# Two leftover expert jobs: six of their eight weight slices go from native FP32 matmuls to split operands, with both parts of the activation side by side

## The chip, the cores and the metric

One core of a Trainium2 chip runs the whole kernel. The metric is the device time of one launch in microseconds; three runs of the kernel before gave 592.71, 593.57 and 594.28. The trace comes from one profiled execution of its own.

## The reference, cut to what matters

A block-wise linear attention gives 1536 rows of 512 values. A first mixture of 8 experts sends each row to its best expert, a second one sends each row to its two best. An expert is `h = max(x @ w1, 0)`, then `out[mask] += weight * (h @ w2)`, with `w1` 512x1024 and `w2` 1024x512 in FP32:

```python
for e in range(E):
    for k in range(2):
        mask = top2[:, k] == e
        h = np.maximum(x[mask] @ w1[e], 0.0)
        out[mask] += top2_w[mask, k, None] * (h @ w2[e])
```

## The kernel before, in words

Behind the attention, the work is a list of 18 jobs: one expert with a fixed number of rows each (its columns, `c`). Jobs 0 to 7 are the first mixture (184 to 224 columns), jobs 8 and 9 take 256 rows of experts 0 and 1 of the second, and the rest of these two experts, 160 columns each, are the **leftover jobs**, which stand as job 10 and job 14 in the order. Jobs 11, 12, 13 and 15 have 416, 408, 400 and 392 columns, jobs 9, 16 and 17 multiply by rows.

A job has 8 steps, one for each 128 of the 1024 hidden units. Steps are numbered through, s = 8 j + f, so job 10 is steps 80 to 87 and job 14 steps 112 to 119. Step s emits, in this order: the hidden product h(s) (`hstep`: four matmul groups, one for each 128 of the 512 inputs, d = 0 to 3) with its relu; the output product y(s-2) (`ystep`, LAG = 2); in f = 1 the copy of the finished output of the job before (`ycopy`); weight loads (`wload`, issued from ACT's queue); the transposes of the next job's rows (`xprep`, in f = 4 to 7 for a job of four blocks, block b = d) and the scaled output rows of the job before (`post2`, `put_rows`); last the split of the weights of step s+3 (`split`, LEAD = 3). Each engine takes its instructions in this order.

Split operands: `split` writes the high part of a weight slice rounded to fp32r (h1, h2: two ACT copies of 128x512) and the rest in bf16 (l1, l2: two DVE subtractions). `xprep` and `hstep` do the same with x (xs) and with the hidden values (hs): high part first, low part behind it in one tile of 2c columns. A product is then high weight times high part, high weight times low part and low weight times the high part in bf16. In `high`, with `side` false the first two are two matmuls of c columns, each with its own weight load; with `side` true they are one matmul of 2c columns, whose two halves must be added afterwards. Before, `side` is true for the output products of jobs 0 to 7 alone, where `ycopy` adds the halves (L810, L811).

The leftover jobs have all eight steps in `raw`: no split, weights straight from the load buffer (r), x as FP32 (xf), native FP32 matmuls (L740), and one ACT relu (hf, L757). The h tile in PSUM has two buffers, so h(s) starts only when the readers of h(s-2) are done; y tiles have one each. When `wload` may refill a load buffer that a leftover job uses is worked out in lines 1216 to 1219 from the raw steps: three steps later than elsewhere, since the last raw slice of a half is read by y(s) two steps on.

Of the kernel before, what the change touches and what calls it, by code (L numbers as in the profile page):

```python
# [8 lines left out]
FT = mybir.dt.float32  # L9
# [5 lines left out]
AF = mybir.ActivationFunctionType  # L15
# [13 lines left out]
KD = DM // 128  # L29
NF = F // 128  # L30
STAT1 = (224, 224)
RANK1 = (224, 216, 208, 200, 192, 184)
EARLY2 = 256
STAT2 = (416, 416)
# [4 lines left out]
CR = max(STAT2[:2]) - EARLY2  # L39
# [11 lines left out]
NJOIN = 2  # L51
OUT_ROWS = N + TRASH
RAWB = 3
LAG = 2
LAST = 3
LEAD = 3
# [29 lines left out]
class Job:  # L86


    def __init__(self, ly, c, e=None, r=None, t0=0, row=False, raw=()):
        self.ly, self.e, self.r, self.t0, self.c, self.row = ly, e, r, t0, c, row  # L90
        self.raw = raw
        self.nt = -(-c // 128)
        self.wr = (W1R, W2R)[ly]

# [5 lines left out]
def emit(ctx, tc, kq, kv, lam, moe_expert_emb, moe_tau, moe_w1, moe_w2, moe2_w_gate, moe2_w_noise,  # L100
         moe2_noise, moe2_w1, moe2_w2, out):
    nc = tc.nc
# [187 lines left out]
    JOBS = [Job(0, c, e=e) for e, c in enumerate(STAT1)]  # L290
    JOBS += [Job(0, c, r=r) for r, c in enumerate(RANK1)]
    JOBS += [Job(1, EARLY2, e=e, row=True) for e in range(2)]
    rest = [Job(1, c, r=r, row=c <= ROWS) for r, c in enumerate(RANK2)]
    rest += [Job(1, STAT2[e] - EARLY2, e=e, t0=EARLY2 // 128, raw=range(NF)) for e in range(2)]
    JOBS += [rest[i] for i in ORDER2]
    NJ = len(JOBS)
    NSTEP = NJ * NF
# [3 lines left out]
    def wload(u, eng=nc.sync):  # L301
# [15 lines left out]
        f0 = half * 512  # L317
        r1 = wts.tile([128, KD, 512], FT, name="r1", bufs=RAWB)
        eng.dma_start(r1, w1[e].rearrange("o (k p) f -> p (o k) f", p=128)[:, :, f0:f0 + 512])
        r2 = wts.tile([128, 4, DM], FT, name="r2", bufs=RAWB)  # L320
        eng.dma_start(r2, w2[e].rearrange("o (k p) f -> p (o k) f", p=128)[:, f0 // 128:f0 // 128 + 4])
# [5 lines left out]
    def drip(n=1):  # L327
        for _ in range(min(n, len(small))):
            fn, *a = small.pop(0)
            fn(*a)  # L330

    def split(s):
# [10 lines left out]
        h1 = wts.tile([128, KD, 128], FR, name="h1", bufs=LEAD + 1)  # L343
        h2 = wts.tile([128, DM], FR, name="h2", bufs=LEAD + 2 + LAG)
        l1 = wts.tile([128, KD, 128], BF, name="l1", bufs=LEAD + 1)
        l2 = wts.tile([128, DM], BF, name="l2", bufs=LEAD + 2 + LAG)
        nc.scalar.activation(h1, a1, AF.Copy)  # L347
# [211 lines left out]
    XS = {}  # L559
# [88 lines left out]
    mo = moe.enter_context(tc.tile_pool(name="mo", bufs=2))  # L648
# [5 lines left out]
    def table1():  # L654

        pr = pm.tile([128, 512], FT, name="t", bufs=2)
        for i in JOIN:
            pa, pb = RR[i]
            nc.tensor.matmul(pr[:, :E * NT], pa, pb, start=i == JOIN[0], stop=i == NTI - 1)
        nc.vector.tensor_add(tab1, tab1, pr[:, :E * NT].rearrange("p (e t) -> p e t", t=NT))  # L660
        window_index(0, tab1[:, :S1, :T1], g1[:, :S1], ok1[:, :S1])
        gather(1)
        gather(0)
        window1(slice(0, S1))
# [71 lines left out]
    def products(c, ops, side=False, low_first=False):  # L736

        if ops[0][2] is None:
            for o, w, _, mov, first, last in ops:
                nc.tensor.matmul(o[:, :c], w, mov, start=first, stop=last, skip_group_check=True)  # L740
            return
        a, b = (low, high) if low_first else (high, low)
        for op in ops:
            a(c, op, side, op[4], False)
        for op in ops:
            b(c, op, side, False, op[5])

    def hstep(s):
        j, f = divmod(s, NF)
        jb = JOBS[j]  # L750
        c = jb.c
        h1, l1, _, _ = SPLIT[s]
        ph = pm.tile([128, 512], FT, name="h", bufs=2)
        if l1 is None:
            products(c, [(ph, h1[:, d, :], None, XS[j][1][:, d, :c], d == 0, d == KD - 1) for d in range(KD)])
            hf = mo.tile([128, CR], FT, name="hf", bufs=LAG + 1)
            nc.scalar.activation(hf[:, :c], ph[:, :c], AF.Relu)  # L757
            HS[s] = hf[:, :c]
            drip(2)
            return  # L760
        products(c, [(ph, h1[:, d, :], l1[:, d, :], XS[j][0][:, d, :], d == 0, d == KD - 1) for d in range(KD)])
        hs = mo.tile([128, 2 * C2], FR, name="hs", bufs=LAG + 2)
        hh, hl = hs[:, :c], hs[:, c:2 * c]
        HS[s] = hs[:, :2 * c]
        nc.scalar.activation(hh, ph[:, :c], AF.Relu)  # L765
        nc.vector.scalar_tensor_tensor(hl, ph[:, :c], 0.0, hh.bitcast(FT), op0=OP.max, op1=OP.subtract)  # L766
        drip()

    def row_product(s, t):
        j, f = divmod(s, NF)  # L770
        _, _, h2, l2 = SPLIT[s]
        hh, hl = (HS[s][:, o + t * 128:o + (t + 1) * 128] for o in (0, JOBS[j].c))
        nc.tensor.matmul(PY[j][t], hh, h2, start=f == 0, stop=False)  # L773
        nc.tensor.matmul(PY[j][t], upper_half(hh), l2, start=False, stop=False)  # L774
        nc.tensor.matmul(PY[j][t], hl, h2, start=False, stop=f == NF - 1)  # L775

    def ystep(s):
        j, f = divmod(s, NF)
        if f == 0:
            PY[j] = [pm.tile([128, 512], FT, name=f"y{d}") for d in range(KD)]  # L780
        _, _, h2, l2 = SPLIT[s]
        w = [slice(d * 128, (d + 1) * 128) for d in range(KD)]
        ops = [(PY[j][d], h2[:, w[d]], None if l2 is None else l2[:, w[d]], HS[s],
                f == 0, f == NF - 1) for d in range(KD)]
        if JOBS[j].row:
            last = s >= NSTEP - LAST
            if last and f < NF - 1:
                return
            for t in range(JOBS[j].nt):
                for x in range(s - LAST + 1 if last else s, s + 1):  # L790
                    row_product(x, t)
                if last:
                    put_rows(j, t, PY[j][t], 128)
        else:
            products(JOBS[j].c, ops, not JOBS[j].ly, low_first=True)
        del SPLIT[s], HS[s]

    def ycopy(j):
        jb = JOBS[j]
        c = jb.c  # L800
        if jb.row:
            for t in range(jb.nt):
                put_rows(j, t, PY[j][t], 128)
            return
        yt = yts.rearrange("p (d c) -> p d c", d=KD) if jb.ly else yt1
        YT[j] = yt
        for d in range(KD):
            o = yt[:, d, :c]
            if not jb.ly:
                nc.scalar.activation(o, PY[j][d][:, c:2 * c], AF.Copy)  # L810
                nc.vector.tensor_add(o, PY[j][d][:, :c], o)  # L811
            elif d % 2:
                nc.scalar.activation(o, PY[j][d][:, :c], AF.Copy)
            else:
                nc.vector.tensor_copy(o, PY[j][d][:, :c])  # L815
# [209 lines left out]
    def put_rows(j, t, src, p):  # L1025

        w, ix = Q[j]
        row = mo.tile([128, DM], FT, name="orow", bufs=4)
        if t % 2:
            nc.scalar.activation(row[:p], src[:p], AF.Copy, scale=w[:p, 0, t:t + 1])  # L1030
        else:
            nc.vector.tensor_scalar(row[:p], src[:p], w[:p, 0, t:t + 1], None, op0=OP.mult)  # L1032
        nc.gpsimd.memset(spacer, 0.0)
        s = nc.gpsimd.indirect_dma_start(  # L1034
            out=out[:, :], out_offset=bass.IndirectOffsetOnAxis(ap=ix[:p, t:t + 1], axis=0),
            in_=row[:p], in_offset=None, compute_op=OP.add)
        for o in scat3.setdefault(j, []):
            tc.declare_no_dep(s.ins, o.ins, reason="rows of other tokens")
        scat3[j].append(s)
# [176 lines left out]
    for u in range(len(WLOADS), 2 * NJ):  # L1216
        raw = [f % 4 for f in JOBS[(u - 3) // 2].raw if f // 4 == (u - 3) % 2 and u >= 3]
        s = max(0, 4 * (u - 3) + max([WF] + [x + LAG for x in raw]))
        loads.setdefault(s, []).append(u)

    table1()
    for s in range(NSTEP + LAG):
        j, f = divmod(s, NF)
        if s < NSTEP:
            hstep(s)

        if s >= LAG and not (f == LAG and 0 < j <= E):
            if f == LAG + 1 and 0 < j <= E:
                ystep(s - LAG - 1)
            ystep(s - LAG)  # L1230
        if f == LAG - 1 and j and not (j == NJ and JOBS[-1].row):
            ycopy(j - 1)
        for u in loads.get(s, ()):
            wload(u, nc.scalar)
        if 12 <= s < 12 + 4 * 8 and s % 4 == 0:
            zero_out(s // 4 - 3)
        for fn, a in sorted(todo.get((j, f), ()), key=lambda x: (post1_e, pe_0, pe_1).index(x[0]) if x[0] in (post1_e, pe_0, pe_1) else 3):
            if fn in stages:
                drip(99)
            fn(*a)  # L1240
        split(s + LEAD)
# [225 lines left out]
```

## Time and profile before

| what | us |
| --- | --- |
| median of three runs | 593.57 |
| profiled execution, whole | 598.39 |
| its span, first to last instruction | 596.6 |
| PE busy | 570.7 |
| DVE busy | 379.5 |
| ACT busy | 294.9 |
| mean granted TensorE clock | 0.984 |

A row of the timeline has the start in us from the span's start, the time, engine, line, operation, tiles and shape. Times of one instruction run from its start to its end in the pipeline; the next on the same engine often starts sooner, so the cost of one in a row of many is the distance between two starts. L740 counts two instructions for one FP32 matmul: a group "x8" is the four products of one step.

### The profile page before, as it was taken

Reading aid. Unit: us, or ns where it says so; the run is one execution under the profiler, and the core shown is the slowest. Engines: PE = TensorE matmul, PEld = TensorE weight load, DVE = VectorE, ACT = ScalarE, POOL = GpSimd, SP = SyncE. Lnnn points to the kernel's source line nnn. Section 1 sums busy time; section 2 is a strip of 40 time slices with the busy share of each in tenths; the row PEclk is TensorE's granted clock in tenths of the full one; section 3 lists DMA queues with packets and bytes.
Section 4 is the critical chain, followed back from the end, with each engine's and each line's share of the span. In section 5 each row is a group of like instructions: output and inputs, shape, how many; then the busy total and the mean of one; then the engine's idle time right before and its main releaser. Section 6 shows DMA issues by size and latency. Waiting matters only on the chain.

```text
span 596.6 us, 11448 instructions
## 1 busy us (share of the span) xinstructions
PE 570.7 (96%) x4216; PEld 482.8 (81%) x4217; DVE 379.5 (64%) x1162; ACT 294.9 (49%) x696; POOL 211.3 (35%) x408
## 2 busy tenths in 40 slices
PE   5999779999999999999999999999999999999992
PEld 3898669999999998897778887887879988777761
DVE  3688759788888888878851644665632364655520
ACT  3566326776677667676531534435331444435310
POOL 5786434423624523233355131032132613031303
PEclk9899799999999999999999999999999999999997
DMA  6999139867787775765687585165435776261404
GB/s 215 377 301 388 76 101 373 314 228 254 282 316 251 253 264 178 264 232 178 213 236 203 192 301 185 28 170 182 149 49 197 187 257 203 103 176 20 53 1 57
DMA packets 56353, 119.40 MB, mean 200 GB/s; under 512 B 4973, under 2 KB 6549, under 8 KB 56290
## 3 DMA queue, kind: packets, MB, share of 16 engines
q10 hardware_dynamic: 38208, 75.60, 36.2%
q0 software_dynamic: 9360, 25.38, 16.5%
q1 hardware_dynamic: 8722, 17.62, 8.5%
q8 instruction: 35, 0.57, 0.4%
q14 instruction: 28, 0.23, 0.1%
HBM read 100.50 MB, written 18.09 MB: 199 GB/s over the span
## 4 chain that ended last, share of the span: by engine, by line
PE 86%; DMA 4%; DVE 3%; POOL 1%; ACT 1%; issue 1%; SPq 1%; POOLq 0%; DVEq 0%
PE h L729 12%; PE h L730 11%; PE h L734 10%; PE y L727 8%; PE y L734 8%; PE y L730 4%; PE y L729 4%; PE t L710 4%; PE h L740 3%; PE y L740 3%; PE y L774 2%; PE y L775 2%; PE y L773 2%; DMA xw<-x,g 2%; PE px L431 2%; PE pa L376 2%
## 5 line engine op out<-in xcount | busy, mean ns | idle before, releaser
L729 PE MATMUL h<-xs,h 128*128 128x224 f32 (+11 forms) x512 | 148.6, 314 | 0.0
L730 PE MATMUL h<-xs,h 128*128 128x224 f32 (+11 forms) x512 | 142.1, 301 | 0.0
L1034 POOL DMA_INDIRECT out_dram<-orow,ix x30 | 47.9, 1596 | 202.3 <-DVE orow L1032 137.8
L349 DVE TENSOR_TENSOR l<-r,h 128x512 bf16<-128x512 f32 x128 | 88.9, 695 | 31.2 <-ACT h L347 29.7
L765 ACT ACTIVATE hs<-h 128x224 fp32r<-128x224 f32 (+11 forms) x128 | 51.8, 405 | 98.7 <-PE h L734 98.5
L730 PEld LDWEIGHTS h<-xs,h 128*128 128x128 f32 x512 | 97.3, 190 | 1.6 <-DVE xs L715 0.5
L734 PEld LDWEIGHTS <-l 128*128 128x128 bf16 x896 | 74.0, 97 | 29.9 <-issue 8.3
L729 PEld LDWEIGHTS h<-xs,h 128*128 128x128 f32 x512 | 97.1, 190 | 1.2
L766 DVE SCALAR_TENSOR_TENSOR hs<-h,hs 128x224 fp32r<-128x224 f32 (+11 forms) x128 | 57.6, 450 | 49.5 <-ACT hs L765 49.1
L734 PE MATMUL h<-xs,l 128*128 128x224 bf16 (+11 forms) x512 | 87.0, 291 | 0.0
L351 DVE TENSOR_TENSOR l<-r,h 128x512 bf16<-128x512 f32 x125 | 85.4, 684 | 0.0
L347 ACT ACTIVATE h<-r 128x512 fp32r<-128x512 f32 x128 | 79.8, 624 | 6.8 <-DVE yt L815 2.7
L348 ACT ACTIVATE h<-r 128x512 fp32r<-128x512 f32 x128 | 79.4, 621 | 1.4 <-DMA r<-in_moe_w_dram 1.4
L727 PE MATMUL y<-hs,h 128*128 128x448 f32 (+5 forms) x256 | 64.2, 372 | 0.0
L734 PE MATMUL y<-hs,l 128*128 128x224 bf16 (+9 forms) x384 | 62.2, 283 | 0.0
L715 DVE TENSOR_TENSOR xs<-t,xs 128x384 fp32r<-128x384 f32 (+8 forms) x42 | 24.6, 588 | 58.9 <-ACT xs L714 58.8
L714 ACT ACTIVATE xs<-t 128x384 fp32r<-128x384 f32 (+8 forms) x42 | 21.5, 516 | 57.4 <-PE t L710 52.7
L729 PE MATMUL y<-hs,h 128*128 128x416 f32 (+3 forms) x128 | 49.1, 384 | 0.0
L775 PE MATMUL y<-h,hs 128*128 128x512 f32 x80 | 46.7, 583 | 0.0
L730 PE MATMUL y<-hs,h 128*128 128x416 f32 (+3 forms) x128 | 44.3, 346 | 0.0
L727 PEld LDWEIGHTS y<-hs,h 128*128 128x128 f32 x256 | 42.6, 189 | 0.9
L773 PE MATMUL y<-h,hs 128*128 128x512 f32 x80 | 34.8, 435 | 0.0
(266 smaller groups left out, 920.2 us busy)
## 6 DMA issues: line engine op xcount, KB each, us to landing
r<-in_moe_w_dram ACTq DMA_DIRECT2D x68, 1024.0 KB, 5.2
kq<-in_kq_dram SPq DMA_DIRECT2D x12, 512.0 KB, 6.1
kv<-in_kv_dram SPq DMA_DIRECT2D x12, 512.0 KB, 6.8
x<-row POOLq DMA_DIRECT2D x8, 517.0 KB, 8.2
r<-in_moe_w_dram SPq DMA_DIRECT2D x4, 1024.0 KB, 11.2
out_dram<-zeros ACTq DMA_DIRECT2D x7, 512.0 KB, 4.6
x<-xr POOLq DMA_DIRECT2D x11, 265.0 KB, 5.5
MT<-zpad SPq DMA_DIRECT2D x2, 256.0 KB, 4.4
```

The source lines that it names most:

```text
L347: nc.scalar.activation(h1, a1, AF.Copy)
L348: nc.scalar.activation(h2, a2, AF.Copy)
L349: nc.vector.tensor_sub(l1, a1, h1.bitcast(FT))
L351: (nc.gpsimd if s < LEAD else nc.vector).tensor_sub(l2, a2, h2.bitcast(FT))
L727: nc.tensor.matmul(o[:, :2 * c], hi, mov, start=first, stop=last, skip_group_check=True)
L729: nc.tensor.matmul(o[:, :c], hi, mov[:, :c], start=first, stop=False, skip_group_check=True)
L730: nc.tensor.matmul(o[:, :c], hi, mov[:, c:], start=False, stop=last, skip_group_check=True)
L734: nc.tensor.matmul(o[:, :c], lo, upper_half(mov[:, :c]), start=first, stop=last, skip_group_check=True)
L765: nc.scalar.activation(hh, ph[:, :c], AF.Relu)
L766: nc.vector.scalar_tensor_tensor(hl, ph[:, :c], 0.0, hh.bitcast(FT), op0=OP.max, op1=OP.subtract)
L775: nc.tensor.matmul(PY[j][t], hl, h2, start=False, stop=f == NF - 1)
L1034: s = nc.gpsimd.indirect_dma_start(out=out[:, :], out_offset=bass.IndirectOffsetOnAxis(ap=ix[:p, t:t + 1], axis=0), in_=row[:p], in_offset ...
```

## The change

A job gets a pair `side`: for its hidden product, and for its output product. The leftover jobs get true for both, jobs 0 to 7 keep true for the output alone. Of the leftover jobs' steps, only f = 0 and f = 4 stay in `raw`; f = 1, 2, 3, 5, 6 and 7 are split, with matmuls of 320 columns on the high weights. Behind the hidden product, ACT copies the second half out of PSUM (hx), DVE adds it onto the first half in PSUM, and then come the relu and the subtraction that give hs. `ycopy` adds halves for the leftover jobs too.

```diff
+RAWREST = (0, 4)
...
+        self.side = bool(raw), bool(raw) or not ly
...
-    rest += [Job(1, STAT2[e] - EARLY2, e=e, t0=EARLY2 // 128, raw=range(NF)) for e in range(2)]
+    rest += [Job(1, STAT2[e] - EARLY2, e=e, t0=EARLY2 // 128, raw=RAWREST) for e in range(2)]
...
-        products(c, [(ph, h1[:, d, :], l1[:, d, :], XS[j][0][:, d, :], d == 0, d == KD - 1) for d in range(KD)])
+        side, _ = jb.side
+        products(c, [(ph, h1[:, d, :], l1[:, d, :], XS[j][0][:, d, :], d == 0, d == KD - 1) for d in range(KD)], side)
+        if side:
+            hx = mo.tile([128, CR], FT, name="hx")
+            nc.scalar.activation(hx[:, :c], ph[:, c:2 * c], AF.Copy)
+            nc.vector.tensor_add(ph[:, :c], ph[:, :c], hx[:, :c])
...
-            products(JOBS[j].c, ops, not JOBS[j].ly, low_first=True)
+            products(JOBS[j].c, ops, JOBS[j].side[1], low_first=True)
...
-            if not jb.ly:
+            if jb.side[1]:
                 nc.scalar.activation(o, PY[j][d][:, c:2 * c], AF.Copy)
                 nc.vector.tensor_add(o, PY[j][d][:, :c], o)
```

Through lines 1217 and 1218 the shorter `raw` also moves four weight loads three steps ahead: in job 10 those of steps 85 and 89 to 82 and 86, in job 14 those of steps 117 and 121 to 114 and 118. Through `xstart` and `xprep` the leftover jobs get xs as well as xf.

## Rows read from the trace of the kernel before

**Rows 1.** Busy time by stretch: length, PE, PEld, DVE, ACT, POOL, clock, DMA, GB/s.
```profile
59.50:62.40 2.90, 0.06 (x1) 0.00 (x0) 2.76 (x5) 0.13 (x1) 2.58 (x4) 1.00 0.68 266
62.40:69.20 6.80, 6.39 (x36) 5.58 (x37) 5.97 (x21) 2.21 (x5) 2.12 (x6) 0.50 0.05 21
315.00:336.00 21.00, 21.00 (x143) 19.02 (x141) 6.62 (x21) 6.53 (x16) 8.71 (x14) 1.00 0.79 235
```

**Rows 2.** Timeline of PE in job 10 and at job 11's start.
```profile
320.62 1.25 PE L740 MATMUL h<-xf,r 128*128 128x160 f32 x8
321.70 1.25 PE L740 MATMUL y<-hf,r 128*128 128x160 f32 x8
...
335.76 0.66 PE L710 MATMUL t<-ident,xw 128*128 128x128 f32 x4
336.36 0.46 PE L729 MATMUL h<-xs,h 128*128 128x416 f32 x1
...
337.78 0.35 PE L730 MATMUL h<-xs,h 128*128 128x416 f32 x1
...
338.72 0.57 PE L740 MATMUL y<-hf,r 128*128 128x160 f32 x3
```

**Rows 3.** Timeline of PE at the end of job 7: 184 columns.
```profile
262.54 0.50 PE L734 MATMUL h<-xs,l 128*128 128x184 bf16 x4
262.88 0.49 PE L734 MATMUL y<-hs,l 128*128 128x184 bf16 x4
263.15 0.92 PE L727 MATMUL y<-hs,h 128*128 128x368 f32 x4
263.90 0.28 PE L729 MATMUL h<-xs,h 128*128 128x256 f32 x1
264.02 0.28 PE L730 MATMUL h<-xs,h 128*128 128x256 f32 x1
```

**Rows 4.** Groups of ACT and DVE by form: busy us, mean ns, idle before.
```profile
L757 ACT ACTIVATE hf<-h 128x160 f32<-128x160 f32 x16 | 4.8, 301 | 19.6 <-PE h L740 19.6
L811 DVE TENSOR_TENSOR yt<-y,yt 128x184 f32<-128x184 f32 x4 | 1.1, 332 | 0.0
L1030 ACT ACTIVATE orow<-t,ws 128x512 f32<-128x512 f32 x4 | 2.8, 689 | 7.4 <-PE t L1022 7.4
```

**Rows 5.** Timeline of ACT in jobs 9 to 11, idle before in brackets.
```profile
314.46 0.38 ACT L765 ACTIVATE hs<-h 128x256 fp32r<-128x256 f32 x1 [1.28 <-PE h L734]
...
333.59 0.52 ACT L714 ACTIVATE xs<-t 128x416 fp32r<-128x416 f32 x1 [1.13 <-PE t L710]
334.01 0.62 ACT L347 ACTIVATE h<-r 128x512 fp32r<-128x512 f32 x1
334.53 0.62 ACT L348 ACTIVATE h<-r 128x512 fp32r<-128x512 f32 x1
...
338.92 0.52 ACT L765 ACTIVATE hs<-h 128x416 fp32r<-128x416 f32 x1 [0.90 <-PE h L734]
```

**Rows 6.** Timeline of DVE in step 86.
```profile
334.14 0.59 DVE L715 TENSOR_TENSOR xs<-t,xs 128x416 fp32r<-128x416 f32 x1 [1.06 <-ACT xs L714]
334.66 0.69 DVE L349 TENSOR_TENSOR l<-r,h 128x512 bf16<-128x512 f32 x1
335.27 0.68 DVE L351 TENSOR_TENSOR l<-r,h 128x512 bf16<-128x512 f32 x1
```

**Rows 7.** Timeline of ACT: a weight load in step 89.
```profile
343.35 0.31 ACT L813 ACTIVATE yt<-y 128x160 f32<-128x160 f32 x1 [0.24 <-PE y L740]
343.85 0.38 ACTq L319 DMA_DIRECT2D r<-in_moe_w_dram  x1
344.40 0.39 ACTq L321 DMA_DIRECT2D r<-in_moe_w_dram  x1
```

**Rows 8.** Timeline of ACT in step 114 and of PE in step 120.
```profile
459.98 0.30 ACT L757 ACTIVATE hf<-h 128x160 f32<-128x160 f32 x1 [0.58 <-PE h L740]
...
477.32 0.35 PE L730 MATMUL h<-xs,h 128*128 128x392 f32 x1
```

## The prediction

> **What bounds the kernel now.** I read the busy time by stretch first, then PE's timeline through job 10, then ACT and DVE over the same steps, then single forms. From 315 to 336 us, which is job 10, PE is busy for all of the 21.00 us; DVE works 6.62 and ACT 6.53 [rows 1]. So the leftover jobs are bound by PE alone, and the elementwise engines have 14 us to spare. The change takes PE time out of just these jobs and pays in ACT and DVE time. The question is whether the spare time lies where the new work has to be done, in a fixed order, each piece behind another.
>
> **What PE saves.** A native group starts at 320.62 and the next at 321.70: 1.08 us [rows 2], so 2.16 for h and y of one step. The nearest side-by-side group has 184 columns: y from 262.88 to 263.90, 1.02 us for four low products of 184 and four high ones of 368 [rows 3]. For 160 and 320 columns 4x24 + 4x48 columns go; high products of 256 columns, loads included, follow each other in 0.12 us [rows 3], so the weight loads don't yet set the rate, and at 2.4 columns a ns I take off 0.12: 0.90. For h, high first: four of 320 at 0.145 (between 0.12 for 256 and the 0.75/4 of the 368 group, which includes a change of weights) is 0.58; low 0.34 less 0.04 is 0.30 [rows 3]; 0.88. A split step saves 0.20 + 0.18 = 0.38, twelve of them 4.6 us.
>
> The Trainium skill ("TensorE: Matmul & The Clock Gate", section "Back-to-back issue gap") gives a lone matmul's gap as its columns / 2.4 plus 2.5 ns: 136 ns for 320, 69 for 160, so an estimate of 1.64 us a step and a gain of 6.3 us. This trace has 120 ns for 256 columns where the rule gives 109, so the measurement decides and 4.6 stands.
>
> **What ACT and DVE get.** Each split step adds two copies and two subtractions of 128x512 for the split, a copy hx, an add, a subtraction for hs. Distances between starts: split copies 0.52, x copy to split copy 0.42 [rows 5]; subtractions 0.61, x subtraction to split subtraction 0.52 [rows 6]. From an ACT end to the DVE start on its result 0.03 (334.11 to 334.14) [rows 5, 6]; from the end of an h group on PE (338.72) to ACT's start 0.20 (338.92) [rows 2, 5]. hx and relu are 0.30 each, as L757 at 160 columns [rows 4], and hold ACT 0.20 (a split copy of 0.62 lets the next start after 0.52). The add writes PSUM, which no row does; the nearest, L811, adds out of PSUM at 184 columns in 0.33 [rows 4]. I take 0.32; its bounds are 0.30, the ACT copy of the same shape, and 0.69, a 512-column subtraction [rows 6].
>
> In queue order these make a ring: DVE's add of step s+1 stands behind the split subtractions issued in step s, these behind ACT's split copies, these behind the relu, and the relu behind the add of step s. One pass, add to add: add and hand-over 0.35, relu 0.20, split copy to DVE 0.65, two subtractions 1.22: **2.42 us** against 1.78 of PE for a split step. Before, a leftover relu waited for nothing but PE. With an x copy on ACT (steps 85 to 87) a pass is 2.84.
>
> **The weight loads moved.** In step 82 two DMA issues stand on ACT between relu and split copies, in step 86 two and the reading of the expert's number. Two issues take from 343.85 to 344.79, 0.94, plus 0.15 to the first; with the number 1.44 from the start of the instruction ahead (343.35) [rows 7]. The passes become 3.31 and 4.08. Before, these loads stood in steps 85 and 89, with no ring behind them. The transfers themselves start earlier and cost nothing; splits seven steps later need them.
>
> **Job 10 added up.** h(82) starts 0.20 before its 320.62 (h(81) is shorter): 320.42. Plus 0.88, 0.20 and hx 0.33: the add of 82 at 321.83. Passes: 82 3.31, 83 2.42, 84 (native: x subtraction 0.52 and two subtractions 1.22) 1.74, 85 2.84, 86 4.08: add of 87 at 336.22. Then add and hand-over 0.35, relu 0.20, the x copy of block 3 0.52 + 0.03 and its subtraction 0.59 + 0.03: ready for PE at 337.94.
>
> PE from 320.42: steps 82 to 87 take 1.96, 1.78, 2.58, 2.38, 2.56, 2.38 (y of the native steps falls into 82 and 86; transposes 0.60 each from 335.76 to 336.36 [rows 2] in 84 to 87), 13.64 in all. It would start h(88) at 334.06 and its eighth high product, the low part of x block 3, 1.42 later (336.36 to 337.78 [rows 2]), at 335.48. **It waits there about 2.5 us for that subtraction.** The eighth product stands at 337.94 instead of 337.78: +0.16. Behind it y(86) and y(87) save 0.36. Job 10 comes out at -0.2.
>
> **Job 14.** hx(114) starts where relu stood, 459.98 [rows 8], less 0.40 for two shorter h groups: 459.58, the add at 459.91. The same passes, and job 13's row scalings: in 115 and 117 on ACT 0.59 each (0.69 long [rows 4], less 0.10), in 116 about as much on DVE; that of 114 fits under ACT's weight load. 3.31, 3.01, 2.33, 3.43, 4.08, then 1.72: ready at 477.8 instead of 477.32 [rows 8]. +0.5, less 0.36: +0.1.
>
> **Edits at nothing.** The extra x parts of job 10 (two more ACT copies, two DVE subtractions in step 78) fall into 1.28 us of idle ACT before 314.46 [rows 5]; uncovered, they would cost up to 0.9. `ycopy`'s four copies and adds after the last y take some 1.3 us, while PE does the next h group of 416 columns, over 2.3 us (336.36 to 338.72 [rows 2]); uncovered, 0.5 more than now.
>
> **Sum.** -4.6 of PE work, +4.5 of new waits, in the two jobs' accounts -0.2 and +0.1: -0.1 us. The profiled execution had 598.39 (span 596.6), 4.8 above the median of the runs; both move alike, so 598.3 there and 593.5 on the median of 593.57. Bounds: no waits at all, -4.6; the add at 0.69, which costs 0.37 in each of ten ring passes, +3.6.
>
> **Rivals.**
> *A, the spare time hides it.* The ring isn't closed because PE's slack of two steps (h has two PSUM buffers) swallows it, as the 14 us spare would suggest: the full 4.6 is kept, 589.0; with passes 0.2 shorter than I work out, 2.0 of it, 591.5. For it: ACT and DVE at a third of the stretch [rows 1]. Against it: only six steps, no time to catch up before x block 3.
>
> *B, the ring is dearer: slower than before.* Each 0.1 us more on a pass costs 1.0 over ten passes; from 0.19 on it leaves what I call no change. Reason: the add reads and writes the PSUM bank that ACT reads before and after, and no row shows such a hand-over. With 0.3 it is +2.9: 596.4. Against it: hand-overs out of PSUM are 0.03 here.
>
> *C, the clock falls in the new waits.* With PE nearly idle from 59.50 to 62.40 (0.06 busy), the granted clock of the following 6.80 us was 0.50, the 1.2 GHz level [rows 1]: 3.4 us of work lost. Two waits of 2.5 us are a little shorter than that idle of 2.9. One fall is 596.9, two 600.3. The Trainium skill ("TensorE: Matmul & The Clock Gate", section "What's actually happening") says that the clock is set by how busy the PE recently was, so a stall can cost again after it ends; the trace agrees, by the half clock for 6.80 us behind that idle.
>
> *D, it isn't done*: the halves could be run as before, with no time changed; the code leaves it little room.
>
> **How the numbers follow.** About 0.3%, 1.8 us, is what a measurement here can tell from none. The forecast, own range 592 to 595.3, 0.47; A 0.21; B 0.17; C 0.12; D 0.03. Forecast and D are "same": 0.50; A "faster" 0.21; B and C "slower" 0.29. The range goes from half of A (590.4) to one fall of the clock or B's upper part (597.4), leaving out A's full gain and C twice.
>
> **What would show it.** Right: L740 with a quarter of its matmuls; high groups of 320 columns 0.14 to 0.15 apart; hx 0.30, the add near 0.32; DVE adds of neighbouring split steps 2.4 to 4.1 apart; PE waits of some 2 us for an xs subtraction ahead of the eighth high product of steps 88 and 120, none above 0.5 elsewhere; clock 1.0 behind them. Step by step wrong: no PE wait there (A); adds further apart with the same forms (B); a stretch at 0.5 (C). The loads' place on ACT would be the wrong step if the passes of 82 and 86 were no longer than 83 and 85.

## The result, and the profile after

The changed kernel took 597.85 us (median of 11 runs, 596.42 to 601.73), the kernel before 594.28 (11 runs beside it, 592.64 to 596.29). The ratio is 1.0076, with a 95% interval of 1.0059 to 1.0093: slower, by 3.6 us in the medians (the ratio stands for some 4.5), where no change (593.5) was forecast, and just outside the range (597.4).

The profiled execution after has a span of 596.0 us against 596.6 before, and that difference says nothing: ahead of the leftover jobs the execution before lost time to half-clock stretches (step 4 begins at 93.50 us in it, at 89.93 after). So I set both traces equal where the h group of step 76 starts on PE, and compare the starts of later groups. After minus before, in us:

| start of h in step | 82 | 83 | 88 | 89 | 92 to 113 | 120 | 121 | 123 to the end |
|---|---|---|---|---|---|---|---|---|
| | -0.12 | +1.29 | -0.04 | +2.29 | +2.05 | +0.24 | +3.16 | +2.87 |

Read it as a bill. Job 10 gains 0.12 by step 82, loses 1.41 between 82 and 83, gains 1.33 by 88, loses 2.33 at 88 and gains 0.24 behind it: +2.05. Job 14 gains 1.81, loses 2.92 at step 120, gains 0.29: +0.82. The remaining 0.7 of the 3.6 is not in this execution; what the runs say of it comes below.

Busy time by stretch, after (length, PE, PEld, DVE, ACT, POOL, clock, DMA, GB/s); the first row answers to the last of [rows 1]:

```profile
315.00:336.00 21.00, 17.86 (x133) 15.28 (x131) 14.80 (x42) 11.40 (x30) 8.64 (x12) 1.00 0.74 228
332.90:336.90 4.00, 2.14 (x9) 1.41 (x8) 3.29 (x9) 3.11 (x8) 0.00 (x0) 1.00 0.96 323
```

Before, these 21 us were job 10; after, the work stands 3.42 us earlier, so they hold nearly all of job 10 and the start of step 88. PE, which left no gap before, has 3.14 us of idle in them, 1.45 at y(80) and 1.69 at step 88, and DVE has gone from 6.62 to 14.80. The lower row is the start of step 88: PE works 2.14 of 4.00 us, at full clock in this execution; step 120 looks the same. What PE waited for from 88 to 585 us, after (waited for: us in total, times, longest); before, none of these three is there:

```profile
PE h L732 <- ACT xs L717: 3.5, 2, 1.8
PE y L743 <- DVE orow L1040: 1.5, 1, 1.5
...
PE h L733 <- DVE xs L718: 0.5, 3, 0.2
```

The first and third are the forecast waits for x block 3 at h(88) and h(120). The second was not forecast: the native y(80), the first writer of an output bank in job 10, waits for DVE's row scaling of job 9, the last reader of that bank. PE's timeline in job 10, after (start, us):

```profile
317.08 0.75 PE L730 MATMUL h<-xs,h 128*128 128x320 f32 x4
317.66 0.46 PE L737 MATMUL h<-xs,l 128*128 128x160 bf16 x4
...
319.58 1.35 PE L743 MATMUL y<-hf,r 128*128 128x160 f32 x8 [1.45 <-DVE orow L1040]
320.66 0.86 PE L730 MATMUL h<-xs,h 128*128 128x320 f32 x4
321.37 0.46 PE L737 MATMUL h<-xs,l 128*128 128x160 bf16 x4
321.67 0.45 PE L737 MATMUL y<-hs,l 128*128 128x160 bf16 x4
...
322.58 1.25 PE L743 MATMUL h<-xf,r 128*128 128x160 f32 x8
...
333.94 0.35 PE L733 MATMUL h<-xs,h 128*128 128x416 f32 x1
335.98 0.45 PE L732 MATMUL h<-xs,h 128*128 128x416 f32 x1 [1.69 <-ACT xs L717]
336.61 0.46 PE L733 MATMUL h<-xs,h 128*128 128x416 f32 x1 [0.17 <-DVE xs L718]
```

The h group from 320.66 to 321.67 takes 1.01, y to 322.58 takes 0.91. The wait at h(88) lies at the seventh and eighth high products. Where y(80)'s wait comes from stands on ACT in step 78; the later rows are the weight loads in steps 82, 86 and 114, after:

```profile
309.06 0.57 ACT L717 ACTIVATE xs<-t 128x480 fp32r<-128x480 f32 x1 [2.56 <-PE t L713]
310.35 0.57 ACT L720 ACTIVATE xf<-t 128x480 f32<-128x480 f32 x1 [0.72 <-DVE xs L718]
...
311.51 0.30 ACT L720 ACTIVATE xf<-t 128x160 f32<-128x160 f32 x1 [0.39 <-DVE xs L718]
311.71 0.62 ACT L350 ACTIVATE h<-r 128x512 fp32r<-128x512 f32 x1
...
319.95 0.38 ACTq L322 DMA_DIRECT2D r<-in_moe_w_dram  x1
321.08 0.38 ACTq L324 DMA_DIRECT2D r<-in_moe_w_dram  x1
...
330.76 0.30 ACT L773 ACTIVATE hs<-h 128x160 fp32r<-128x160 f32 x1 [0.89 <-DVE h L769]
331.26 0.38 ACTq L322 DMA_DIRECT2D r<-in_moe_w_dram  x1
332.15 0.38 ACTq L324 DMA_DIRECT2D r<-in_moe_w_dram  x1
332.57 0.52 ACT L717 ACTIVATE xs<-t 128x416 fp32r<-128x416 f32 x1 [1.51 <-issue]
...
459.63 0.84 ACTq L324 DMA_DIRECT2D r<-in_moe_w_dram  x1
```

The x parts of job 10, 0.77 us of ACT in two copies before, are now a chain from 309.06 to 311.81, 2.75 us: ACT's copy to FP32 (xf) waits each time for DVE's subtraction. The two share no result; both read the same transposed block in PSUM, which an experiment below takes up. The split copies begin only behind it. DVE, after:

```profile
317.86 0.31 DVE L769 TENSOR_TENSOR h<-h,hx 128x160 f32<-128x160 f32 x1
...
318.78 0.74 DVE L1040 TENSOR_SCALAR orow<-y,ws 128x512 f32<-128x512 f32 x1
319.44 0.33 DVE L769 TENSOR_TENSOR h<-h,hx 128x160 f32<-128x160 f32 x1
323.45 0.32 DVE L769 TENSOR_TENSOR h<-h,hx 128x160 f32<-128x160 f32 x1
...
327.56 0.33 DVE L769 TENSOR_TENSOR h<-h,hx 128x160 f32<-128x160 f32 x1
...
330.40 0.33 DVE L769 TENSOR_TENSOR h<-h,hx 128x160 f32<-128x160 f32 x1
...
334.86 0.33 DVE L769 TENSOR_TENSOR h<-h,hx 128x160 f32<-128x160 f32 x1
...
335.96 0.59 DVE L718 TENSOR_TENSOR xs<-t,xs 128x416 fp32r<-128x416 f32 x1
...
458.55 0.33 DVE L769 TENSOR_TENSOR h<-h,hx 128x160 f32<-128x160 f32 x1 [1.01 <-ACT hx L768]
...
462.39 0.33 DVE L769 TENSOR_TENSOR h<-h,hx 128x160 f32<-128x160 f32 x1
...
467.73 0.33 DVE L769 TENSOR_TENSOR h<-h,hx 128x160 f32<-128x160 f32 x1
...
471.13 0.32 DVE L769 TENSOR_TENSOR h<-h,hx 128x160 f32<-128x160 f32 x1
...
475.33 0.33 DVE L769 TENSOR_TENSOR h<-h,hx 128x160 f32<-128x160 f32 x1
```

Splits, the add of step 81 and its hs stand ahead of the row scaling at 318.78, and ahead of those, from 315.11 to 316.7, twelve small operations select job 10's output rows. The scaling ends at 319.52, and y(80) starts at 319.58. The adds that follow are those of steps 82, 83, 85, 86 and 87: passes of 4.01, 4.11 (two steps, one of them native), 2.84 and 4.46. The last five are those of steps 114, 115, 117, 118 and 119 in job 14: 3.84, 5.34, 3.40 and 4.20. The new forms, after (busy us, mean ns, idle before):

```profile
L743 PE MATMUL y<-hf,r 128*128 128x160 f32 x32 | 5.2, 306 | 1.5 <-DVE orow L1040 1.5
L769 DVE TENSOR_TENSOR h<-h,hx 128x160 f32<-128x160 f32 x12 | 3.9, 326 | 2.2 <-ACT hx L768 2.2
L768 ACT ACTIVATE hx<-h 128x160 f32<-128x160 f32 x12 | 3.6, 296 | 2.6 <-PE h L737 2.6
```

A quarter of the native products is left (32 of 128), and the two pieces that no row of before showed cost what was taken, 0.33 and 0.30.

### The profile page after: what moved, and what is told of

Same layout as the page of the kernel before. It is cut to its first block, busy times and chain, and to the rows that moved or that the text cites. A ratio compares the mean times of both kernels' runs of the same rounds, so it can differ in the third digit from the quotient of the medians.

```text
span 596.0 us, 11568 instructions
## 1 busy us (share of the span) xinstructions
PE 568.8 (95%) x4216; PEld 476.8 (80%) x4217; DVE 400.4 (67%) x1218; ACT 311.1 (52%) x740; POOL 212.7 (36%) x408
## 4 chain that ended last, share of the span: by engine, by line
PE 79%; DVE 8%; DMA 5%; ACT 3%; issue 2%; POOL 1%; SPq 1%; ACTq 1%; POOLq 0%; DVEq 0%
PE h L732 11%; PE h L733 11%; PE h L737 10%; PE y L730 9%; PE y L737 8%; PE y L733 4%; PE y L732 4%; PE t L713 3%; PE y L782 2%; PE y L783 2%; PE y L781 2%; DVE l L354 2%; PE px L434 2%; PE po L401 2%; PE t L874 1%
## 5 line engine op out<-in xcount | busy, mean ns | idle before, releaser
L352 DVE TENSOR_TENSOR l<-r,h 128x512 bf16<-128x512 f32 x140 | 96.3, 688 | 34.0 <-ACT h L350 33.1
L773 ACT ACTIVATE hs<-h 128x224 fp32r<-128x224 f32 (+12 forms) x140 | 55.3, 395 | 105.2 <-PE h L737 93.6
L354 DVE TENSOR_TENSOR l<-r,h 128x512 bf16<-128x512 f32 x137 | 93.7, 684 | 0.0
L737 PE MATMUL h<-xs,l 128*128 128x224 bf16 (+12 forms) x560 | 92.6, 286 | 0.0
L350 ACT ACTIVATE h<-r 128x512 fp32r<-128x512 f32 x140 | 87.4, 625 | 9.8 <-DVE hs L774 3.7
L774 DVE SCALAR_TENSOR_TENSOR hs<-h,hs 128x224 fp32r<-128x224 f32 (+12 forms) x140 | 61.6, 440 | 44.3 <-ACT hs L773 43.6
L351 ACT ACTIVATE h<-r 128x512 fp32r<-128x512 f32 x140 | 87.0, 622 | 0.0
L730 PE MATMUL y<-hs,h 128*128 128x448 f32 (+6 forms) x304 | 74.2, 366 | 0.0
L737 PE MATMUL y<-hs,l 128*128 128x224 bf16 (+10 forms) x432 | 67.6, 277 | 0.0
L718 DVE TENSOR_TENSOR xs<-t,xs 128x384 fp32r<-128x384 f32 (+10 forms) x46 | 26.6, 579 | 50.0 <-ACT xs L717 49.5
L717 ACT ACTIVATE xs<-t 128x384 fp32r<-128x384 f32 (+10 forms) x46 | 23.2, 508 | 58.9 <-PE t L713 52.4
L730 PEld LDWEIGHTS y<-hs,h 128*128 128x128 f32 x304 | 49.7, 189 | 0.9
```

Of the source, the lines that this page charges most:

```text
L351: nc.scalar.activation(h2, a2, AF.Copy)
L352: nc.vector.tensor_sub(l1, a1, h1.bitcast(FT))
L354: (nc.gpsimd if s < LEAD else nc.vector).tensor_sub(l2, a2, h2.bitcast(FT))
L730: nc.tensor.matmul(o[:, :2 * c], hi, mov, start=first, stop=last, skip_group_check=True)
L737: nc.tensor.matmul(o[:, :c], lo, upper_half(mov[:, :c]), start=first, stop=last, skip_group_check=True)
```

## The experiments

My theory after this: two new waits of the ring at x block 3, which the loads' place on ACT feeds, and one for job 9's row scaling, which the x parts of step 78 and the small operations feed; and, for the part that the profile does not hold, the clock. The rivals: the loads cost by their transfers and not by their place; the new pieces on PE are dear by themselves; the falls of the clock are chance. All kernels start from the changed one. Ratios are to the kernel before, beside which each ran; "trace" is the end of the leftover jobs in the one profiled execution, against before, by the alignment above. Of that end, 0.03 to 0.47 us stands already at h(80), behind the transposes of step 78, which wait 0.2 to 0.6 us for the DMA of job 10's rows, in another amount in each execution; so a few tenths between two traces say nothing.

**The loads of the ring on Sync's queue.**
```
-            wload(u, nc.scalar)
+            wload(u, nc.sync if u in (22, 23, 24, 25, 30, 31, 32, 33) else nc.scalar)
```


> The eight half-job weight loads around the two leftover jobs are issued by the Sync engine instead of ACT; their steps and transfers stay. Ring theory: the passes of steps 82 and 86 lose what the issues hold ACT (about 0.9 and 1.2 us each time), PE's waits for x block 3 ahead of steps 88 and 120 shrink from about 2.3 and 2.9 to 1.0 and 1.5 us, the kernel gets about 2.6 us shorter than the changed one and stands about 1 us above the one before; the 1.5 us wait of y(80) stays. Rival: it is the earlier transfers themselves (traffic) that cost; then moving the issue to another engine changes nothing.


Measured: 592.79 against 594.67, 0.9969 (0.9953 to 0.9985); trace -0.29, 3.2 less than the changed kernel. PE's waits:
```profile
PE y L743 <- DVE orow L1040: 1.4, 1, 1.4
...
PE h L732 <- ACT xs L717: 0.5, 1, 0.5
...
PE h L733 <- DVE xs L718: 0.3, 2, 0.2
```
and DVE's adds of steps 85, 86 and 87:
```profile
324.94 0.33 DVE L769 TENSOR_TENSOR h<-h,hx 128x160 f32<-128x160 f32 x1
...
327.77 0.32 DVE L769 TENSOR_TENSOR h<-h,hx 128x160 f32<-128x160 f32 x1
...
330.61 0.33 DVE L769 TENSOR_TENSOR h<-h,hx 128x160 f32<-128x160 f32 x1
```
The pass of step 86 is now 2.84, like that of 85, instead of 4.46: the issues' place on ACT was the price. The same bytes move, so the transfers are not. The wait at x block 3 is nearly gone, that of y(80) untouched: they are two things. The load of step 82 gave nothing by itself: the pass is 2.81 instead of 4.01, but the next two take 5.29 instead of 4.11, since ACT now waits there for PE, which y(80) had held up. About 1 us above the kernel before was expected, and it is 1.9 below. The trace gained 3.2 where 2.6 was expected; the rest of the time is not in it. The mean granted clock of these runs is 0.9912 against 0.9893 before, worth some 1.1 us (an estimate, 0.0019 of 596 us), and why it is higher is not shown.

**Step 7 native as well: five split steps.**
```
-RAWREST = (0, 4)
+RAWREST = (0, 4, 7)
```


> Step 7 of the leftover jobs is native as well (0, 4, 7). Ring theory: the last pass before x block 3 then has no copy, add and second wait, so both waits ahead of steps 88 and 120 go nearly altogether: 4 to 4.5 us shorter than the changed kernel, 1.0 to 1.5 us shorter than the one before, with the wait of y(80) left. Rival: the time is lost in the side-by-side products or in a dearer add, spread over all split steps; then one native step fewer on each job gives back at most a sixth of it, 0.5 us, less the 0.38 of PE time that it costs.


Measured: 592.15 against 594.67, 0.9959 (0.9940 to 0.9977); trace -1.61. The only one of the three waits that is left:
```profile
PE y L743 <- DVE orow L1040: 1.4, 1, 1.4
```
With step 7 native, its split in step 84 and its own pass of the ring are gone, and ACT and DVE reach x block 3 in time, though one step's PE saving is given up in each job. The wait at block 3 was worth more than that, so the rival, products that are dear in every split step, falls. The time gained 2.5 us where 1.0 to 1.5 was expected, the trace 1.6.

**Job 10's row selection nine steps later.**
```
-            put(*((j, 0) if j < E + 3 else (j - 1, 7)), fn, j)
+            put(*((j + 1, 1) if j == E + 2 and fn is sel2 else (j, 0) if j < E + 3 else (j - 1, 7)), fn, j)
```


> The twelve small DVE operations that select job 10's output rows move from step 80 to step 89. Theory of a second queue: y(80) waits for a PSUM bank whose reader, job 9's row scaling, stands on DVE behind these operations and behind the add of step 81; without them the 1.5 us wait falls to 0.2 or less, the kernel gets 1.3 to 1.5 us shorter than the changed one, and the waits ahead of steps 88 and 120 stay at 2.3 and 2.9. Rival: the bank is late because of the add of step 81 alone; then the wait stays above 1 us.


Measured: 598.97 against 594.67, 1.0078 (1.0050 to 1.0106); trace +3.46. The expected gain is not in the time. In the trace it is there and then lost: y(80) waits no more, h(88) starts 1.39 ahead of before instead of 0.04, but h(89) is 2.16 behind. The stretch of the wait, and the one behind it:
```profile
333.00:335.20 2.20, 0.49 (x3) 0.19 (x1) 1.77 (x4) 1.31 (x5) 0.00 (x0) 1.00 1.02 391
335.90:339.30 3.40, 3.40 (x15) 2.69 (x16) 3.09 (x20) 1.88 (x4) 0.00 (x0) 0.59 0.63 243
```
PE was busy for 0.49 of 2.20 us, and the granted clock then fell to its 1.2 GHz level (mean 0.59 over these 3.40 us). That made rival C, the clock, the thing to test.

**No side-by-side h in the leftover jobs, y as changed.**
```
-        self.side = bool(raw), bool(raw) or not ly
+        self.side = False, bool(raw) or not ly
```


> The hidden product of the leftover jobs' split steps is not side by side: two loads of the high weights, both parts summed on PE, no copy hx, no add; the output product stays side by side. Ring theory: a pass falls from 2.42 to about 1.8 us, below PE's time, which rises by about 0.33 us a split step; no wait ahead of steps 88 and 120, and the wait of y(80) falls to 0.3. About 3 us shorter than the changed kernel, 0 to 0.6 us shorter than the one before. Rival: the split copies and subtractions alone overload ACT and DVE; then the waits ahead of steps 88 and 120 stay above 1.5 us and the kernel is slower than the changed one.


Measured: 593.74 against 594.67, 0.9986 (0.9968 to 1.0005); trace -0.55. The ring loses hx and the add, and the waits at block 3 go, with y(80)'s down to 0.2; PE pays the second load of the high weights. It comes out even: the interval holds no change.

**Five split steps, and the late selection.** Both edits above.


> Steps 0, 4 and 7 native and the twelve small operations moved: neither the wait ahead of steps 88 and 120 nor the one of y(80). Ring theory with the second queue: 1.3 us below the kernel with 0, 4, 7 native alone, 3.3 to 4 us below the one before (590.5 to 591.5 on 594.5). Rival: the waits are symptoms and PE's saving is itself overrated; then it stays within 0.5 us of the kernel with 0, 4, 7 alone.


Measured: 590.43 against 593.86, 0.9944 (0.9924 to 0.9964); trace -3.16; none of the three waits is left. This is faster than both kernels. The selection's place, worth nothing in time while the other wait stood, is now worth some 1.5 us in the trace (-3.16 against -1.61); in time it is 0.9 us, and the two intervals overlap.

**The late selection with eight spare matmuls at the start of steps 88 and 120.** They write the h bank, which the first product then clears, and keep PE busy.
```
+        if j and not f and JOBS[j - 1].raw:
+            for _ in range(8):
+                nc.tensor.matmul(ph, ones, warm, start=True, stop=True)
```


> As the kernel with the late small operations, plus eight matmuls of zeros (128x512 bf16, some 1.7 us in all, each overwritten by the real product) on PE at the start of steps 88 and 120, where it waited 2.2 and 2.6 us; they add nothing to the result. Clock theory: PE no longer stands idle there, the granted clock stays at 2.4 GHz behind the waits, and although PE does more the kernel gets 1.5 to 3.5 us shorter than the one without the filler (about 596 on a before of 594.5), with the mean granted clock up from 0.985 towards 0.991. Rival: the half clock in that one trace was chance; then the time is the same or up to 0.5 us longer.


Measured: 594.84 against 593.86, 1.0017 (0.9997 to 1.0037); trace +1.13. Against the same kernel without the spare matmuls (1.0078, in another set of runs) the time falls by 0.6%, though PE has more to do. In the traces the two are 2.33 apart; some 0.7 of that is not the clock but the load in step 114, whose pass took 3.39 here and 4.13 there. The stretches around step 88:
```profile
331.50:335.00 3.50, 3.28 (x15) 1.97 (x15) 2.74 (x6) 2.61 (x7) 0.00 (x0) 1.00 0.95 318
335.00:339.00 4.00, 3.83 (x24) 2.95 (x24) 3.69 (x21) 2.21 (x5) 0.00 (x0) 1.00 0.65 253
```
Full clock throughout. Over the runs the mean granted clock went from 0.9845 to 0.9905; before had 0.9893 and 0.9897 in these sets. So the falls belong to the waits. Of all eleven profiles, those told below included, four have both long waits at block 3, and four of these eight waits were followed by half clock; in the other seven the clock is 1.00 from 328 to 345 and from 466 to 485 us.

**The FP32 copy of an x block ahead of the split one.**
```
+        if jb.raw:
+            nc.scalar.activation(XS[j][1][:, d0:d1, :c], v, AF.Copy)
         if len(jb.raw) < NF:
...
-        if jb.raw:
-            nc.scalar.activation(XS[j][1][:, d0:d1, :c], v, AF.Copy)
```


> In the x preparation of the leftover jobs ACT reads the transposes for the FP32 copy first and for the high part second, so that ACT's second read of a PSUM bank no longer stands behind DVE's read of the same bank. Theory: the 1.5 us wait of y(80) comes from this serial chain in step 78, which pushes the splits of steps 78 to 80 and all behind them on DVE; it falls to about 0.3, the kernel gets 1.2 to 1.3 us shorter than the changed one and the waits ahead of 88 and 120 stay (and with them the risk of a half clock). Rival: the order of the two copies doesn't matter, the amount does; then the wait stays above 1 us.


Measured: 597.57 against 593.86, 1.0059 (1.0032 to 1.0086); trace +4.41. The order of two copies takes y(80)'s wait from 1.5 us to none (expected 0.3): read together, ahead of DVE, the four copies no longer wait, which is what the shared PSUM block explains. Without the twelve small operations the same wait was gone too, so it needed both. The ring shows the same: the add of step 82, 7.16 us behind h(80) in the first profile of the changed kernel, comes 6.23 behind it in both (h(80) at 312.96 with the late selection, at 310.12 here), where it now waits for hx and not for DVE:
```profile
319.19 0.33 DVE L769 TENSOR_TENSOR h<-h,hx 128x160 f32<-128x160 f32 x1 [0.53 <-ACT hx L768]
...
316.35 0.33 DVE L769 TENSOR_TENSOR h<-h,hx 128x160 f32<-128x160 f32 x1 [0.33 <-ACT hx L768]
```
In time it is 2.9 us below the changed kernel of the same set (600.42, next experiment), where 1.2 to 1.3 was expected, and no faster than the changed kernel of the first set (+3.7 against +3.6 on the kernel before), so the runs do not settle what it is worth. In this execution both waits at block 3 were followed by half clock, as behind step 88:
```profile
332.30:335.80 3.50, 3.32 (x11) 1.95 (x12) 3.11 (x21) 1.70 (x5) 0.00 (x0) 0.51 0.86 331
```

**The changed kernel once more,** beside the three before it, with no edit.


> The changed kernel once more, beside the others on the same chip: 0.6 to 0.9% above the one before; waits of 1.5, 2.3 and 2.9 us at y(80), ahead of 88 and ahead of 120. Clock theory: in some executions the granted clock halves behind one of the two long waits, so the mean granted clock of its runs is below that of the kernels without the waits (0.987 against 0.991). Rival: no difference in mean clock.


Measured: 600.42 against 593.86, 1.0111 (1.0086 to 1.0136); trace +5.08. Its waits agree with those of the first profile within 0.1, but here the clock fell behind the wait of step 120:
```profile
477.60:481.00 3.40, 3.40 (x15) 3.03 (x14) 3.16 (x17) 1.53 (x3) 0.00 (x0) 0.50 1.02 397
```
This is the same program as that of the first profile, with and without a fall. The two agree within 0.4 up to h(120) (+0.59 against +0.24); the end is +5.08 against +2.87. At the eighth product of step 120, ahead of the fall, they are 0.64 apart: 0.24 stood already at h(80), and the pass of step 114 took 4.25 here and 3.84 there. So the fall costs about 1.6 us, near the 1.7 that 3.4 us at half clock lose. The mean granted clock of the runs is 0.9865 against 0.9897 before, as expected; the time, 1.1% above the kernel before, is more than the 0.6 to 0.9% expected.

**Six split steps with the causes removed:** loads on Sync, the late selection, and the x parts of jobs 11 and 15 one step earlier.
```
-        x0, *xs = (XG5, XG6, XG7)[j - E] if j < E + 3 else (3, 4, 5, 6, 7)
+        x0, *xs = (XG5, XG6, XG7)[j - E] if j < E + 3 else (2, 3, 4, 5, 6) if JOBS[j - 1].raw else (3, 4, 5, 6, 7)
```


> Six split steps as in the change, but the ring is relieved where it hurt: the eight weight loads are issued by Sync, job 10's small operations stand in step 89, and the x preparation of jobs 11 and 15 runs one step earlier (steps 83 to 86 and 115 to 118 instead of 84 to 87 and 116 to 119). Ring theory: no PE wait above 0.7 us around either job, no half clock, and PE keeps 3 of its 4.6 us: 0.5% (3 us) below the kernel before. Rival: with 16 split passes ACT and DVE can't keep up whatever the order; then waits of more than 1 us come up at steps 89, 90, 121 or 122 and the kernel stays within 1 us of the one before.


Measured: 590.80 against 593.81, 0.9951 (0.9929 to 0.9974); trace -2.87. What is left of the waits of the ring, in step 122:
```profile
PE h L732 <- DVE hs L774: 0.5, 1, 0.5
```
The saving of the twelve split steps is real and is kept once the three waits are gone. This version and the one with five split steps can't be told apart (590.80 and 590.43); both beat both kernels.

## Why the prediction was wrong

It set -4.6 us of PE work against +4.5 of waits. In the profile without a fall of the clock the changed kernel is at +2.87 and not at -0.1. Since PE waits for x block 3 at the end of both jobs, what counts is when that block is ready, so the error is found along the ring. By the alignment the two traces are 3.42 us apart here: the block of job 10, worked out for 337.94, was due at 334.52 in the trace after, and its product started at 336.61, 2.09 late. The 2.09 by steps:

- **"Edits at nothing" failed: 1.03, and some 0.5 more.** The add of step 82 was due at 318.41 and came at 319.44, right behind the row scaling. I had put job 10's extra x parts into 1.28 us of idle ACT and bounded them by 0.9, as two copies and two subtractions side by side. They run in turn, 2.75 us against 0.77, and everything behind them on ACT and DVE is late. The working also let the add start as soon as hx was there, with nothing else on DVE: the twelve small operations of step 80, 1.5 us of DVE's queue, and the row scaling have no term in it. With the small operations moved, or with the x parts no longer in turn, the add comes 6.23 us behind h(80), where the working has 6.16 (321.83 less 315.67); with both in place it is 7.16. I also never asked who waits for DVE in job 10's first steps: job 9's row scaling, and through its bank y(80), 1.45 us. That comes back in the ring, since the second issue of the load in step 82 follows y(80): 1.13 behind the first here, 0.62 and 0.71 in the two kernels in which y(80) didn't wait, where the pass is 3.51 and 3.59 instead of 4.01. The Trainium skill ("PSUM — Partial Sum Buffer", section "PSUM bank collisions raise a hardware error") says that the compiler orders any two instructions of different engines on one bank and quadrant of 32 partitions, ACT and DVE reads too; the trace agrees, with ACT waiting 0.72 and 0.39 us for DVE's subtraction.
- **"The weight loads moved" was right in kind and too cheap: 0.2 and 0.38 in job 10, 0.53 and 0.12 in job 14.** The passes were 4.01 for 3.31 (0.5 of that by y(80)) and 4.46 for 4.08, in job 14 3.84 for 3.31 and 4.20 for 4.08. The price had been read off one load with its issues 0.55 apart [rows 7]; in step 86 they are 0.89 apart, and in step 114 the second lasts 0.84 instead of 0.38. It is no fixed price: the pass of step 114 was 3.39 to 4.25 in the five profiles that keep this load on ACT behind six split steps. That the place on ACT costs, and not the bytes, the first experiment shows. Job 14 has no other miss ahead of step 120: its first add came at 458.55, where the working, moved by the 3.42 and job 10's 2.05, gives 458.54.
- **The rest of the ring was right:** the pass with an x copy 2.84 for 2.84, the two over step 84 4.11 for 4.16, in job 14 5.34 and 3.40 for 5.34 and 3.43. The waits came at the predicted block in both jobs and cost 2.33 and 2.92, where about 2.5 and as much in job 14 were named.
- **"What PE saves" was too large, but nearly without effect.** The y group came out right (0.91 for 0.90), and the low half of h (0.30). The high half of h took 0.71 where 0.58 was taken: 1.92 a step, a saving of 0.24 against the native 2.16 and not 0.38. The four h groups that come right behind split products of the job before do take 0.58 or 0.59 (317.08 to 317.66); the eight behind transposes or native products take 0.67 to 0.71 (320.66 to 321.37). The kernel before has the same difference in its own trace: the first product of a group takes 0.12 behind split products (263.90 to 264.02 [rows 3]) and 0.23 behind transposes (the two rows below). So the sum took its price from the cheaper kind of place; why a place is dearer was not tested. (The 6.3 us named beside the sum should be 6.2: 0.52 twelve times; nothing rests on it.) Ahead of x block 3 a smaller saving only shortens the wait; behind it, y(86), y(87) and their like saved 0.24 and 0.29 instead of 0.36: 0.19 in all.

```profile
312.75 0.39 PE L729 MATMUL h<-xs,h 128*128 128x256 f32 x1
312.98 0.28 PE L730 MATMUL h<-xs,h 128*128 128x256 f32 x1
```

2.09, 0.65 of job 14 and 0.19 are 2.93 of the 2.97 us between +2.87 and -0.1.

**Rival C had too small a chance, 0.12.** I argued that a wait of 2.5 us is shorter than the idle 2.9 us of [rows 1]. Waits of 1.7 us, with PE not even quite idle, were followed by half clock in three of the profiles (late selection, FP32 copy first, the changed kernel again), and not in the first one of the changed kernel. A fall lasted some 3.4 us and cost 1.6, not the 3.4 that the rival took from the longer idle of [rows 1]. Falls in part of the executions fit what the first profile lacks, but do not account for all: the changed kernel is at +3.6 in one set of runs and at +6.6 in the other, with the same mean granted clock, 0.9867 and 0.9865. The two ratios, 1.0076 and 1.0111, have intervals that overlap, and what parts the sets is not shown. The Trainium skill ("TensorE: Matmul & The Clock Gate", section "What's actually happening") says that the moment at which the clock changes is run-variable; the two profiles of the same kernel agree, and why a given execution falls stays open.

**Rival B** named the right sign for the wrong reason: the add cost 0.33, and a pass without a load came out as worked out, not 0.3 dearer. **Rival A** fell: the idle of ACT and DVE did not lie where the ring needs it. D fell by the forms.

So the forecast had the mechanism that decides, the ring, and failed on what enters it: a step that it had costed at nothing, and a load read off a quieter place.

## What to carry to other kernels

Idle time of an engine covers a moved piece of work only if the pieces can run at the same time; two engines that read one PSUM block ran in turn here, so let each engine do all its reads of the block in one go. When work moves to an engine that was idle, list everything already queued there that frees a buffer for the engine that sets the time. A DMA issue on an engine that is part of a ring costs its place in the queue, so give it to an engine outside the ring; and price a wait of the matmul engine together with the chance that its clock falls behind it.

## What the runs showed of the hardware

- Granted clock behind short waits: after 2.20 us with 0.49 us of PE work its mean was 0.59 over the 3.40 us from 335.90 (late selection); after a like wait (2.14 us of PE work in 4.00) in the first profile of the changed kernel it stayed at 1.00. With eight spare matmuls at the start of each such step the clock stayed at 1.00, and the ratio to the kernel before went from 1.0078 to 1.0017.
- Two hardware DMA issues and the reading of the expert's number on ACT put its next instruction 1.81 us behind the start of the one ahead (step 86, 330.76 to 332.57), where 1.44 was read before [rows 7].
- Four products of 320 columns took 0.58 or 0.59 us right behind split products, and 0.67 to 0.71 behind transposes or native products.
